# Four changes of order and three gate operations on GpSimd in an mLSTM and two-layer MoE kernel

## The chip, the cores and the metric

The kernel runs on one core of a Trainium2 chip. The metric is the device time of one execution, in microseconds. The engines are called PE (TensorE), DVE (VectorE), ACT (ScalarE), POOL (GpSimd) and SP (SyncE, here only a queue that issues DMAs).

## The reference

Three layers follow one another on 1536 tokens of width 320 (2 sequences of 768, 8 heads of 40).

```python
# 1. mLSTM: a recurrence over the 768 steps, for every sequence and head
m_new = np.maximum(f_gate[:, :, t] + m, i_gate[:, :, t])
f_stab = np.exp(f_gate[:, :, t] + m - m_new)
i_stab = np.exp(i_gate[:, :, t] - m_new)
C = f_stab * C + i_stab * outer(vt, kt);  n = f_stab * n + i_stab * kt
y[:, :, t] = sigmoid(o_gate) * (C @ qt) / np.maximum(np.abs(n @ qt), 1.0)
# 2. a dense layer with softplus, 320 -> 2048 -> 320
h = x @ w_in;  g = np.maximum(h, 0.0) + np.log1p(np.exp(-np.abs(h)));  x = g @ w_out
# 3. eight experts, one per token, 320 -> 1024 -> 320
e_idx = np.argmax(x @ w_gate, axis=1);  gate_w = softmax(x @ w_gate)[e_idx]
eom = sigmoid(x @ w_output_gate)
out[mask] = gate_w[mask] * eom[mask, e] * (np.maximum(x[mask] @ w1[e], 0.0) @ w2[e])
```

Matmul operands are split in a high and a low part, so most products are three passes over PE.

## The kernel before

The program is recorded by a planner (`Weaver`, L45). Every piece of work is a generator that names, before each group of instructions, the engine it wants (P, A, V, G or S for PE, ACT, DVE, POOL, SP; "AV" for either of two) or the events that it waits for. The planner keeps an estimated clock for each engine, takes the task that can start first (ties by `rank`), and so writes one fixed order of instructions per engine. A change of one engine letter, price or rank can therefore move instructions far away. On the chip each engine runs its own queue in that order and waits for semaphores.

The stages are:

- *Gates* (`gates`, L384). The recurrence of m is a scan along 768 steps on 80 partitions (16 heads, copied at three places). `gates(0, 0, 1)` does chunk 0 (128 steps) and `gates(1, 1, NCH)` chunks 1 to 5, 640 columns at once. With tiles fg, ig and mm it computes fg + mm(t-1) - mm(t), clips it, sums it per chunk into acum, splits acum of chunks 0 and 1 in bf16 parts (tile scratch), computes ig - mm, and transposes both on PE into gps, whose exponentials (gts) are the per-token weights.
- *Attention* (`chunk`, L518), per chunk c and sequence b. ap is the mask of decays, sp the scores, abc the decayed scores (a product on DVE), pv the values (v on POOL scales them), kv the update of the carried state cst, qc what the state gives. num and sm hold the quotient on DVE; POOL multiplies it with the sigmoid (y), PE transposes it (xp) and it becomes the high and low x of the dense layer.
- *Dense layer* (`up1`, `softplus`, `down1`). ph = x w_in per block of 256 tokens and strip of 128 hidden columns, three exponent/log steps on ACT (ab), g, gh and gl, then acc = g w_out. Strips are done in three legs (4, 4 and 8 of 16) so that PE has this work under attention. Weights come as 64-bit words and are put together on DVE (wta), then split (win, wou).
- *Routing* (`route`, L879, `take_row`, L850) of each 256-token block when its acc is complete: the row is added up, its columns 256 to 320 are copied behind it, PE transposes it (x2tp, x2T) and makes the logits (lg). Small DVE operations on tile rsm find the expert; a one-hot gives rank and totals on PE; newp, more_p, cum, room, base place every token in a slot of 128 rows. POOL scatters the rows to DRAM (`scatter`, an indirect DMA).
- *Between the layers*. `fence` (L1219) lets a POOL memset and a DVE copy on tile pad follow the scatters, before the low parts of w2 (w2s) may be written. `get_meta` (L1253) transposes the experts of the slots to one row (esp), casts it to integers (into pad), and PE loads them in registers. `load_rows` reads the slots back on SP's queue (yac, srow), followed by the last w2raw and the next weights.
- *Experts* (`slots`, `up2`, `post`, `down2`). 15 slots of 128 rows, four quarters of the hidden width: ph, hr (ReLU), tp (transposes), flat and hl (high and low part), yp, and the sum yac on DVE. In the last quarter each slot's yac is sent out by an indirect DMA on POOL (out_dram).

PSUM buffers come from rings: `bank` (4 buffers, 2 of them given to the ph ring at the end of attention), `bank_h`, `bank_y`. Nearly every instruction is recorded by one helper, so its line in the profile is L195; rows are told apart by tile names.

## Time and profile before

| what | value |
|---|---|
| median of 3 runs | 457.0 us (455.26 to 460.16) |
| the profiled execution, whole | 456.22 us |
| its span, first to last instruction | 454.5 us |
| PE, DVE, ACT, POOL busy | 94%, 73%, 68%, 29% of the span |
| granted TensorE clock, mean | 0.956 of full speed |
| DMA | 63.49 MB, mean 140 GB/s |

Times in the trace count from the first instruction. A row of a timeline gives start, duration, engine, operation, the tiles written and read, their shapes, and in brackets how long the engine was idle before it and whom it waited for. The profile's instruction spans overlap by some 0.07 us on DVE. A granted clock of 0.50 is 1.2 GHz, 1.00 is 2.4 GHz.

### The profile page before, as it was taken

The page shows a single profiled execution, that of the slowest core. Times are in us where ns is not written, and L with a number is a line of the kernel's source. Part 1 is how long each engine was busy: PE and PEld are TensorE (multiplying, and loading weights), DVE is VectorE, ACT ScalarE, POOL GpSimd, SP SyncE. Part 2 cuts the span into 40 slices and gives each one's busy share as a digit, 9 for nine tenths or more (in the row PEclk, how much of TensorE's full clock was granted, in tenths as well). Part 3 has the DMA queues.
Part 4 walks back from the last instruction along what each step waited for, and adds up shares of the span by engine and source line. Part 5 has one row for each costly group of instructions (what it writes and reads, how often), then busy time and mean ns, then how long its engine had stood idle before and what let it go on. Part 6 is the DMA issues. An engine that isn't in the chain of part 4 may idle for free.

```text
span 454.5 us, 10149 instructions
## 1 busy us (share of the span) xinstructions
PE 425.6 (94%) x3189; PEld 404.0 (89%) x3189; DVE 332.8 (73%) x866; ACT 307.8 (68%) x881; POOL 133.9 (29%) x220
## 2 busy tenths in 40 slices
PE   8669999999979999999999999859999999999994
PEld 7557989999969999999999999717899999999993
DVE  3897888788995999855756656575569659769742
ACT  2549688888857998876867867445673773774430
POOL 3255476466131330010201101114023033051273
PEclk9676999999997999999999999969999999999998
DMA  8859645799147421100100100019146817726021
GB/s 291 343 173 316 201 144 186 218 338 273 67 150 283 157 95 60 59 0 2 36 2 36 36 1 36 36 64 357 46 120 206 290 36 207 271 68 201 26 103 51
DMA packets 31205, 63.49 MB, mean 140 GB/s; under 512 B 3516, under 2 KB 16063, under 8 KB 31152
## 3 DMA queue, kind: packets, MB, share of 16 engines
q1 hardware_dynamic: 29664, 58.46, 39.4%
q0 software_dynamic: 1488, 4.35, 2.6%
q8 instruction: 30, 0.49, 0.4%
q14 instruction: 23, 0.19, 0.1%
HBM read 54.64 MB, written 8.65 MB: 139 GB/s over the span
## 4 chain that ended last, share of the span: by engine, by line
PE 79%; DVE 8%; ACT 7%; issue 3%; DMA 2%; POOL 1%; SPq 0%; POOLq 0%; DVEq 0%; ACTq 0%
PE ph L195 31%; PE acc L195 17%; PE yp L195 10%; PE pv L195 4%; PE sp L195 4%; PE tp L195 3%; DMA w2raw<-in_w_dram 2%; PE kv L195 2%; PE lg L195 2%; ACT ab L195 2%; PE qc L195 2%; PE heat L195 2%; DVE w2s L195 1%; DVE wta L195 1%; ACT w2s L195 1%
## 5 line engine op out<-in xcount | busy, mean ns | idle before, releaser
L195 ACT ACTIVATE ab<-ab 128x256 f32<-128x256 f32 x192 | 77.7, 419 | 2.3
L195 DVE SCALAR_TENSOR_TENSOR g<-ph,ab 128x256 f32<-128x256 f32 x96 | 39.9, 419 | 24.8 <-ACT ab L195 24.2
L195 PE MATMUL ph<-w1s,flat 128*128 x300 | 56.3, 304 | 1.0 <-DVE w1s L195 0.6
L195 PE MATMUL acc<-win,gh 128*128 128x320 f32 x240 | 56.5, 321 | 0.5 <-ACT gh L195 0.5
L195 POOL TENSOR_TENSOR w1s<-w1raw,w1s 64x256 fp32r<-64x256 f32 x32 | 29.2, 938 | 89.3 <-ACT w1s L195 89.3
L195 PE MATMUL yp<-w2s,flat 128*128 x240 | 53.8, 312 | 0.5 <-ACT flat L195 0.5
L195 DVE TENSOR_TENSOR gl<-g,gh 128x256 fp32r<-128x256 f32 x96 | 45.7, 484 | 9.6 <-ACT gh L195 8.5
L195 ACT ACTIVATE ab<-ph 128x256 f32<-128x256 f32 x96 | 36.4, 381 | 18.0 <-PE ph L195 17.7
L195 PEld LDWEIGHTS ph<-w1s,flat 128*128 128x128 f32 x300 | 43.3, 188 | 2.0 <-ACT flat L195 0.9
L195 ACT CAST gh<-g 128x256 fp32r<-128x256 f32 x96 | 38.2, 403 | 7.4 <-DVE g L195 6.7
L195 PE MATMUL ph<-win 128*128 128x256 f32 x250 | 41.8, 291 | 0.0
L195 ACT ACTIVATE hr<-ph 128x256 f32<-128x256 f32 x60 | 23.1, 386 | 27.3 <-PE ph L195 25.9
L195 PEld LDWEIGHTS yp<-w2s,flat 128*128 128x128 f32 x240 | 39.7, 188 | 0.7 <-ACT flat L195 0.7
L195 DVE TENSOR_TENSOR hl<-tp,flat 128x256 fp32r<-128x256 f32 x60 | 25.2, 421 | 20.7 <-ACT flat L195 20.5
L195 PEld LDWEIGHTS acc<-win,gh 128*128 128x128 f32 x240 | 39.1, 191 | 1.2 <-ACT gh L195 1.0
L195 POOL DMA_INDIRECT rows<-row,rsm x12 | 12.6, 1050 | 93.3 <-ACT ab L195 55.6
L195 PE MATMUL acc<-win,gl 128*128 128x320 f32 x120 | 37.6, 314 | 0.0
L195 ACT CAST w2s<-w2raw 128x640 fp32r<-128x640 f32 x32 | 22.4, 727 | 22.0 <-PE yp L195 21.2
L195 PE MATMUL yp<-w2s,hl 128*128 x120 | 37.2, 310 | 0.0
L195 PEld LDWEIGHTS ph<-win 128*128 128x128 f32 x250 | 35.1, 194 | 0.5 <-issue 0.2
L195 PE MATMUL ph<-w1s,x2l 128*128 x180 | 33.5, 294 | 0.0
L195 PE MATMUL acc<-wou,gh 128*128 128x320 f32 x144 | 32.8, 313 | 0.3 <-ACT gh L195 0.3
(190 smaller groups left out, 1087.8 us busy)
## 6 DMA issues: line engine op xcount, KB each, us to landing
w1raw<-in_w_dram SPq DMA_DIRECT2D x32, 384.0 KB, 4.5
wra<-in_w_in_dram SPq DMA_DIRECT2D x16, 704.0 KB, 4.3
w2raw<-in_w_dram SPq DMA_DIRECT2D x32, 320.0 KB, 3.3
abc<-abc_dram SPq DMA_DIRECT2D x4, 1024.0 KB, 8.2
rows<-pad SPq DMA_DIRECT2D x19, 194.0 KB, 6.0
kT<-in_k_t_dram SPq DMA_DIRECT2D x6, 512.0 KB, 5.2
qT<-in_q_t_dram SPq DMA_DIRECT2D x6, 512.0 KB, 6.1
kn<-in_k_dram SPq DMA_DIRECT2D x5, 416.0 KB, 7.3
```

Of the source, the lines that this page charges most:

```text
L195: return fn(*args, **kw)
```

## The change

Five edits:

1. In `gates`, for chunks 1 to 5 (n = 1), the add and the subtract on fg and the subtract on ig go from DVE to POOL. Chunk 0 stays on DVE.
2. In `take_row`, for the last block, the copy of columns 256 to 320 becomes an add of 64 columns on DVE ahead of the row add.
3. In `route`, the negated maximum and the exponentials on ACT (`weigh`) come ahead of the one-hot; rank and totals get a PSUM tile rk of their own, and the warm matmuls of the last block take a buffer of `bank_y`.
4. `fence` also waits for an event that `get_meta` signals when the cast into pad is recorded.
5. In `up2`, in the last quarter, the last three of the 15 slots have rank 7.0 instead of 9.0, so that they come ahead of `down2` (rank 8).

```diff
@@ gates
-        yield "V"
-        DVE.tensor_tensor(out=fg[:, p0:t1], in0=fg[:, p0:t1], in1=mm[:, p0 - 1:t1 - 1], op=ALU.add)
-        yield "V"
-        DVE.tensor_tensor(out=fg[:, p0:t1], in0=fg[:, p0:t1], in1=mm[:, p0:t1], op=ALU.subtract)
+        eng = (DVE, "V") if n == 0 else (POOL, "G")
+        yield eng[1]
+        eng[0].tensor_tensor(out=fg[:, p0:t1], in0=fg[:, p0:t1], in1=mm[:, p0 - 1:t1 - 1], op=ALU.add)
+        yield eng[1]
+        eng[0].tensor_tensor(out=fg[:, p0:t1], in0=fg[:, p0:t1], in1=mm[:, p0:t1], op=ALU.subtract)
...
-        yield "V"
-        DVE.tensor_tensor(out=ig[:, t0:t1], in0=ig[:, t0:t1], in1=mm[:, t0:t1], op=ALU.subtract)
+        yield eng[1]
+        eng[0].tensor_tensor(out=ig[:, t0:t1], in0=ig[:, t0:t1], in1=mm[:, t0:t1], op=ALU.subtract)
@@ take_row
+            if last:
+                DVE.tensor_tensor(out=row[:, t, DM:CCOL], in0=acc[:, 256:DM], in1=row[:, t, 256:DM], op=ALU.add)
             DVE.tensor_tensor(out=row[:, t, 0:DM], in0=acc, in1=row[:, t, 0:DM], op=ALU.add)
-            yield "AV"
-            copy(row[:, t, DM:CCOL], row[:, t, 256:DM])
+            if not last:
+                yield "AV"
+                copy(row[:, t, DM:CCOL], row[:, t, 256:DM])
@@ route
+    def weigh(le, ex, nmx, ssum, done):
+        yield "A"
+        for t in range(TPB):
+            ACT.activation(out=ex[:, t], in_=le[:, t], func=AF.Exp, bias=nmx[:, t:t + 1], accum_out=ssum[:, t:t + 1])
+        W.signal(done)
...
-        lg, ev = yield from bank.get([P, 64], F32, "lg")
+        lg, lg_ev = yield from bank.get([P, 32], F32, "lg")
...
+        rk, ev = yield from bank.get([P, 24], F32, "rk")
+        rank = rk[:, 0:T8].rearrange("p (t e) -> p t e", e=E)
+        tot = rk[:, T8:T8 + E]
...
         tt(lt, le, bc(mx, E), ALU.is_lt)
+        DVE.tensor_scalar(out=nmx, in0=mx, scalar1=-1.0, scalar2=None, op0=ALU.mult)
+        W.add(after(W.cur.out, weigh(le, ex, nmx, ssum, have_ssum)), 0.9)
...
-            warm, wev = yield from bank.get([P, 4, P], F32, "warm")
+            warm, wev = yield from bank_y.get([P, 4, P], F32, "warm")
...
-        DVE.tensor_scalar(out=nmx, in0=mx, scalar1=-1.0, scalar2=None, op0=ALU.mult)
         tt(sel, lo_, ohb, ALU.mult)
         yield "V"
         DVE.tensor_reduce(out=oge, in_=sel, axis=AX.X, op=ALU.add)
+        yield [have_ssum]
         yield "A"
-        for t in range(T2):
-            ACT.activation(out=ex[:, t], in_=le[:, t], func=AF.Exp, bias=nmx[:, t:t + 1], accum_out=ssum[:, t:t + 1])
         ACT.activation(out=ef, in_=oge, func=AF.Exp, scale=-1.0)
+        W.signal(lg_ev)
@@ fence, get_meta
-        yield [scattered]
+        yield [scattered, have_meta]
...
         DVE.tensor_copy(out=meta, in_=esp)
         W.signal(ev)
+        W.signal(have_meta)
@@ up2
                     yield [slot_ready[s]]
+                W.cur.rank = 7.0 if qn == NQ - 1 and s >= NS - 3 else 9.0
```

What the planner makes of it is shown at three places.

DVE, from the scan of chunks 1 to 5 on (mm is the scan's result, abc the decayed scores, sm and num the quotient of chunk 0, wta the weights put together). Before:

```order
L195 SCALAR_TENSOR_TENSOR mm<-fg,mm,ig 80x640
L195 SCALAR_TENSOR_TENSOR wta<-wra,wta 128x704
L195 TENSOR_TENSOR fg<-fg,mm 80x640
L195 SCALAR_TENSOR_TENSOR wta<-wra,wta 128x704
L195 TENSOR_TENSOR abc<-sp,abc 128x4x128 x2
L195 TENSOR_TENSOR fg<-fg,mm 80x640
L195 TENSOR_SCALAR fg<-fg 80x640
L195 TENSOR_TENSOR abc<-sp,abc 128x4x128
L195 SCALAR_TENSOR_TENSOR acum<-scratch,fg 80x128 x5
L195 TENSOR_SCALAR sm<-pv 128x8
L195 TENSOR_TENSOR abc<-sp,abc 128x4x128
```

The same place on DVE in the changed kernel:

```order
L195 SCALAR_TENSOR_TENSOR mm<-fg,mm,ig 80x640
L195 SCALAR_TENSOR_TENSOR wta<-wra,wta 128x704 x2
L195 TENSOR_TENSOR abc<-sp,abc 128x4x128 x3
L195 TENSOR_SCALAR sm<-pv 128x8
L195 TENSOR_SCALAR fg<-fg 80x640
L195 SCALAR_TENSOR_TENSOR sm<-pv,sm 128x8
L195 TENSOR_TENSOR abc<-sp,abc 128x4x128
L195 RECIPROCAL sm<-sm 128x8
L195 SCALAR_TENSOR_TENSOR acum<-scratch,fg 80x128 x5
L195 TENSOR_TENSOR num<-pv,sm 128x8x40
L195 TENSOR_SCALAR sm<-pv 128x8
L195 CAST scratch<-acum 80x128
```

The two fg operations are gone, three score products stand together, and the clip of fg (TENSOR_SCALAR) stands behind an operation on pv.

POOL at the same time (v_217 and v_219 are the values of the two sequences in chunk 0, v_282 or v_284 and v_318 the same with the decay to the chunk's end, which kv needs; y is the product with the sigmoid; win a low part of weights; v_422 and on belong to chunk 1). Before:

```order
L195 COPY v_219<-gts 128x8
L195 TENSOR_TENSOR v_282<-v_217,sm 128x328
L195 TENSOR_TENSOR v_318<-v_219,sm 128x328
L195 TENSOR_TENSOR win<-wta,win 64x128 x2
L195 TENSOR_TENSOR y<-num,y 128x320
L195 TENSOR_TENSOR v_422<-vn_87,gts 128x8x40
L195 COPY v_422<-gts 128x8
L195 TENSOR_TENSOR v_423<-vn_87,gts 128x8x40
L195 COPY v_423<-gts 128x8
L195 TENSOR_TENSOR y<-num,y 128x320
```

The same place on POOL in the changed kernel:

```order
L195 COPY v_219<-gts 128x8
L195 TENSOR_TENSOR fg<-fg,mm 80x640
L195 TENSOR_TENSOR v_284<-v_217,sm 128x328
L195 TENSOR_TENSOR fg<-fg,mm 80x640
L195 TENSOR_TENSOR v_318<-v_219,sm 128x328
L195 TENSOR_TENSOR win<-wta,win 64x128
L195 TENSOR_TENSOR ig<-ig,mm 80x640
L195 TENSOR_TENSOR win<-wta,win 64x128
L195 TENSOR_TENSOR y<-num,y 128x320 x2
L195 TENSOR_TENSOR v_436<-vn_87,gts 128x8x40
```

The fg operations stand ahead of the v products, ig between the weights, and the second y has moved ahead of chunk 1's values.

DVE behind the last routing (rem, esl are the routing's last results, esp the slots' experts, the 1x1 copy is the fence's). Before:

```order
L195 SCALAR_TENSOR_TENSOR esl<-rsm,esl 128x1
L195 TENSOR_TENSOR rem<-rem,cum 128x1
L195 COPY pad<-pad 1x1
L195 TENSOR_TENSOR w2s<-w2raw,w2s 128x2x320
L195 CAST pad<-esp 1x256
```

The same place on DVE in the changed kernel:

```order
L195 SCALAR_TENSOR_TENSOR esl<-rsm,esl 128x1
L195 TENSOR_TENSOR rem<-rem,cum 128x1
L195 CAST pad<-esp 1x256
L195 COPY pad<-pad 1x1
L195 TENSOR_TENSOR w2s<-w2raw,w2s 128x2x320 x7
```

The cast has moved ahead of the fence's copy and of the w2s subtractions.

In the last slots, PE's order before ends with ph (4 of 8 matmuls), yp, the other 4 ph, transposes, yp; in the changed kernel the last ph is complete ahead of the last four yp groups.

## Rows read from the trace of the kernel before

**Rows 1.** The page's busy times: us, share of the span, instructions.

```profile
PE 425.6 (94%) x3189; PEld 404.0 (89%) x3189; DVE 332.8 (73%) x866; ACT 307.8 (68%) x881; POOL 133.9 (29%) x220
```

**Rows 2.** Busy time by stage: us, engines (instructions), granted clock, DMA share, GB/s.

```profile
20.00:30.00 10.00, 8.54 (x68) 8.25 (x66) 9.54 (x25) 6.06 (x15) 2.47 (x2) 0.84 0.49 177
30.00:40.00 10.00, 7.06 (x33) 5.22 (x33) 9.00 (x17) 7.75 (x29) 5.79 (x8) 0.50 1.06 333
...
120.00:140.00 20.00, 16.95 (x121) 16.43 (x120) 18.15 (x38) 12.60 (x33) 3.95 (x4) 0.87 0.31 97
...
150.00:200.00 50.00, 49.88 (x381) 49.68 (x380) 46.01 (x95) 44.47 (x124) 8.92 (x12) 1.00 0.23 76
```

**Rows 3.** Timeline of DVE, 15 to 34 us.

```profile
15.67 1.35 DVE L195 TENSOR_TENSOR fg<-fg,mm 80x640 f32<-80x640 f32 x1
...
17.75 1.27 DVE L195 TENSOR_TENSOR abc<-sp,abc 128x512 f32<-128x512 f32 x2
...
27.99 0.81 DVE L195 TENSOR_TENSOR ig<-ig,mm 80x640 f32<-80x640 f32 x1
...
33.05 0.48 DVE L195 TENSOR_TENSOR num<-pv,sm 128x320 f32<-128x320 f32 x1
```

**Rows 4.** POOL: its timeline, 28 to 35 us, and two tiles (ns min/median/max).

```profile
28.12 2.07 POOL L195 TENSOR_TENSOR win<-wta,win 64x128 fp32r<-64x128 f32 x1 [5.72 <-ACT win L195]
30.27 0.81 POOL L195 TENSOR_TENSOR y<-num,y 128x320 f32<-128x320 f32 x1
...
33.62 1.38 POOL L195 TENSOR_TENSOR y<-num,y 128x320 f32<-128x320 f32 x1
...
L195 POOL TENSOR_TENSOR win<-wta,win x10: 451/799/2067, 21.8 to 189.0; 64x128 fp32r<-64x128 f32 x10
...
L195 POOL TENSOR_TENSOR w1s<-w1raw,w1s x32: 732/792/1256, 142.7 to 410.1; 64x256 fp32r<-64x256 f32 x32
```

**Rows 5.** Timeline of PE, the head and the end of attention.

```profile
18.52 1.65 PE L195 MATMUL kv<-v,kn 128*104 128x82 f32 x8 [4.37 <-issue]
19.97 2.95 PE L195 MATMUL pv<-v,abc 128*128 128x123 f32 x16
...
40.05 1.43 PE L195 MATMUL ph<-win 128*128 128x256 f32 x5
...
135.54 0.90 PE L195 MATMUL xp<-ident,y 128*128 128x128 f32 x3 [3.02 <-POOL y L195]
```

**Rows 6.** Timeline of DVE, the last block's placement.

```profile
297.82 0.17 DVE L195 TENSOR_TENSOR newp<-lg,room 128x8 f32<-128x8 f32 x1 [0.47 <-ACT rsm L195]
...
299.36 0.17 DVE L195 CAST rsm<-rsm 128x2 uint32<-128x2 f32 x1
```

**Rows 7.** Timelines of DVE, PE, SP and ACT, between routing and slots.

```profile
303.61 0.41 DVE L195 CAST pad<-esp 1x256 int32<-1x256 f32 x1
...
308.48 1.00 PE L195 MATMUL xslot<-ident,yac 128*128 128x128 f32 x6
...
309.12 0.40 SPq L195 DMA_DIRECT2D w2raw<-in_w_dram  x1
...
317.06 0.73 ACT L195 CAST w2s<-w2raw 128x640 fp32r<-128x640 f32 x1 [0.85 <-DMA w2raw<-in_w_dram]
```

**Rows 8.** Timelines of PE and POOL, the last slots.

```profile
441.35 0.99 POOL L195 DMA_INDIRECT out_dram<-yac,tki  x1 [0.30 <-issue]
442.35 0.47 PE L195 MATMUL yp<-w2s,flat 128*128 x2
444.28 0.98 POOL L195 DMA_INDIRECT out_dram<-yac,tki  x1 [1.94 <-DVE yac L195]
446.86 0.44 PE L195 MATMUL tp<-ident,hr 128*128 128x128 f32 x2 [0.53 <-ACT hr L195]
447.76 0.56 PE L195 MATMUL yp<-w2s,flat 128*128 x2 [0.46 <-ACT flat L195]
...
449.94 0.98 POOL L195 DMA_INDIRECT out_dram<-yac,tki  x1 [2.10 <-DVE yac L195]
```

More of the change, by code (lines that the diff above doesn't have):

```diff
@@ L897, in route @@
         T2, T8 = TPB, TPB * E
+        have_ssum = Event()
         small, small_ev = yield from sm_ring.get([P, 8 * T2 + 6 * T8 + 4 * E], F32, "rsm")
@@ L908, in route @@
         le, lo_ = lgv[:, :, 0:E], lgv[:, :, E:2 * E]
-        rank = lg[:, 2 * T8:3 * T8].rearrange("p (t e) -> p t e", e=E)
-        tot = lg[:, 3 * T8:3 * T8 + E]
+        rk, ev = yield from bank.get([P, 24], F32, "rk")
+        rank = rk[:, 0:T8].rearrange("p (t e) -> p t e", e=E)
+        tot = rk[:, T8:T8 + E]
         yield "V"
@@ L1216, in mlstm_moe_kernel @@
     flag = pad[0:1, 0:2]
-    clear, last_placed = Event(), Event()
+    clear, last_placed, have_meta = Event(), Event(), Event()
     def fence():
-        yield [scattered]
+        yield [scattered, have_meta]
         yield "G"
@@ L1249, in mlstm_moe_kernel @@
     meta = pad[0:1, 64:64 + 2 * P].bitcast(I32)
-    have_meta, turned_over = Event(), Event()
+    turned_over = Event()
     evals = {}
```

## The prediction

> **What bounds the kernel now.** I read the page's busy times first: PE works 425.6 of the 454.5 us span [rows 1], so all that any change of order can win lies in PE's 29 idle us and in the stretches where its clock is low. The table by stage says where those are [rows 2]. From 20 to 40 us PE is busy 8.54 and 7.06 of each 10 us, at a granted clock of 0.84 and 0.50 of full speed, while DVE is busy 9.54 and 9.00: the head (gates, first chunks) is DVE's. From 120 to 140 us, where attention ends, PE lacks 3.05 us. From 150 to 200 it is busy 49.88 of 50: there a change of order is worth nothing, but what was won earlier is carried through. Two short serial places follow: the routing of the last block with the start of the expert slots (292 to 310 us), and the last slots.
>
> The change is weighed at those four places. The planner writes one order for the whole program, so the gates on another engine reshuffle everything up to the end of attention; behind the last routing the rows on PE differ only among the first slots and the last three.
>
> **Head: the three gate operations.** DVE loses one add of 1.35 us and two 80x640 operations of 0.81 us [rows 3], 2.97 us in all. POOL has no 640-element row. Its smallest times for 128 and 256 elements are 0.451 and 0.732 [rows 4], 2.2 ns an element, so 0.73 + 384 x 0.0022 = 1.58 us each, an estimate; the nearest stretched row is 2.07 us for 128 elements, 4.6 times the smallest, so 7.3 us is the other end. What is behind them? On POOL the first batch's v product now stands between the add and the subtract, the second's behind it; on DVE the max over fg waits for POOL's subtract, and behind it stand the fourth score product, the scans and all of chunk 1's gates. In the old order the add started at 15.67; from there POOL takes 1.58 + 0.8 (a v product, taken as the undisturbed 128x320 row of 0.81) + 1.58, to 19.6.
>
> In DVE's new rows three score products stand where the add stood, so they start 1.28 earlier than 17.75 (the add without its overlap), at 16.5, and the second ends at 17.7. PE's new rows begin with pv instead of the kv that idled 4.37 us until 18.52 [rows 5]. PE therefore starts 0.8 earlier, and this pv (2.95 us in the old trace) ends near 20.6. The max stands behind an operation on that pv, so POOL's 19.6 is hidden, with 1.0 us to spare. But DVE, done with its products at about 18.3, now idles 2.3 us for pv: of its 2.97 us only 0.7 is left. That is the low end of the gain, if the head stays DVE's.
>
> The high end comes from the second batch's y product on POOL. It ran from 33.62 to 35.00, because the division that feeds it came at 33.05 on DVE, behind the acum casts, weight conversion and the ig subtraction. In the new rows that division stands before the casts, and POOL runs both y products back to back: the first ended at 31.08, the second can end at 31.9, or 32.5 if it is stretched to 1.38 again. That is 3.1 or 2.5 us earlier, and PE's first ph (40.05) needs it. With PE's 0.8 on top the high end is 3.9. I take 2.5, the stretched y row, since DVE's conversions fill that stretch in both orders. Between 45 us and the end of attention PE has so little idle time that I let it carry.
>
> At the end of attention [rows 5] PE idles 3.02 us for the last y. The new rows put about as much work before the last transpose xp, but less between the last pv and it, and between that pv's sum and its division DVE has six operations fewer. I cost this at zero, with 3 us either way as bounds: the gap gone, or doubled.
>
> **Routing of the last block.** In the old order the first operation of the placement (newp) idled 0.47 us on the ACT exponentials and started at 297.82 [rows 6]. In the new one ACT starts them after the negated maximum, while DVE still makes the one-hot, and rank and totals have a PSUM bank of their own. The placement can start once the rank matmuls are done and the output gate is reduced, 0.75 us earlier. Against it stands the 64-column add in front of the row add; the small DVE rows here last 0.17 and cost about 0.1 in a stream, and the ACT copies that it replaces were beside PE's transposes. Net 0.65 to 0.75 us; I take 0.7. The same edits in blocks 0 to 4 lie under PE's 49.88 of 50, and the further PSUM bank is taken when the block's transposes have left theirs, so I count nothing there. Scatter, the read-back of the rows and everything that SP issues behind them move by the same 0.7.
>
> **Fence.** In the old order DVE's cast of the slot experts (pad<-esp) ran at 303.61 [rows 7], behind the fence's copy, which waits for the scatter issue, and behind one w2s subtraction. PE then loads the numbers, runs six warm matmuls and only then transposes slot 0 at 308.48. In the new rows the cast stands directly behind the routing, and could run near 301. The seven w2s subtractions still queue behind the fence's copy on DVE and move 0.7 with the scatter. PE would then be free before the rows land, and slot 0 would start about 2.0 earlier (0.7 from the scatter, 1.3 from the cast). What is late next: w2raw for expert 7, issued by SP behind all row loads at 309.12. ACT's cast of it waited 0.85 us and began at 317.06; it stands at the same place in ACT's queue, after slot 4's ReLU, with the next slots behind it. That landing moves only 0.7. I therefore count 0.7 for routing and fence together, and 2.0 as the other end, if PE finds enough work behind the block.
>
> **Last three slots.** The new rows take all ph products ahead of the last four yp groups. That removes PE's two waits of 0.53 and 0.46 us [rows 8]. But POOL issues each output with 0.99 busy and 0.30 between, 1.29 us apart, and it idled in the old order at 444.28. Now four outputs come together, and the first of them stands on DVE behind both hl subtractions. PE: 442.35 (the old yp's place) plus eight ph (1.0), transpose, half a yp, transpose, half a yp ends near 444.7; ACT and DVE then finish the second hl near 445.2, the output's sum at 445.7, POOL 445.98. The fourth issue is at 445.98 + 3 x 1.29 = 449.85, against 449.94. So POOL takes the place of PE: I count zero, with 1.0 less and 0.3 more as bounds.
>
> **Sum.** The profiled execution took 456.22 us, 1.7 outside its span; it lies 0.8 under the median of 457.0 and inside the runs. 456.2 - 2.5 - 0.7 - 0 = 453.0.
>
> **Rivals.** *The head is given back.* PE reaches 45 us early, but the end of attention comes when DVE and ACT are done, and the gap of 3.02 grows by what was won. For it: PE has less work left behind the last pv. Against it: from 45 to 120 us PE was the busy engine. Only routing stays: 456.2 - 0.7 = 455.5.
>
> *More than forecast.* The head wins the high end, 3.9, since PE is busy earlier where its clock stood at 0.50, and the expert slots win 2.0 because the late w2raw blocks ACT while PE has slots in hand. For it: PE lost only some tenths at that block before. Against it: ACT's queue is in order. 456.2 - 3.9 - 2.0 = 450.3.
>
> *Slower: POOL's add is stretched.* The add now lies beside two weight operations of DVE, each with two SBUF inputs. The trace has such a case: the 128-element POOL subtraction at 28.12 took 2.07 us instead of 0.45 beside DVE's two-input operations [rows 4]. At that ratio the add takes 7.3 us and the subtract ends near 25.3, 4.7 after the pv for which DVE waits anyway; DVE's max, the fourth score product, and with it the second pv, the scans and chunk 1 are that much later. The head loses 4.7 - 2.5 = 2.2: 456.2 + 2.2 - 0.7 = 457.7. It decides for slower from a subtract that ends later than 23.8 (20.6 + 2.5 + 0.7). Against it: 640 elements last longer than the DVE work beside them, and the score products read PSUM. The Trainium skill speaks for it: GPSIMD Engine Reference, Key points, says that GpSimd shares its SBUF interfaces with VectorE and contends with instructions of two SBUF inputs. The 2.07 us row agrees; how far 640 elements are stretched no run here shows.
>
> *It does not do what it says:* the new order of the middle loses as much as the head wins, 456.2. I put it with the second case of no gain above.
>
> **Chances.** Forecast 0.50; head given back 0.22; more 0.16; stretched add 0.12. A measurement of this kernel tells about 1% from no change, 4.6 us of the median 457.0. Under 452.4 lie the case of more and, with one time in four, the forecast (its own range 451.3 to 455): 0.16 + 0.5 x 0.25 = 0.29 for faster. Over 461.6 lies only the far end of the stretched add with a gap that doubles, 0.05. Within 1%: 0.66. The range takes in the case of more nearly whole and the stretched add: 450.0 to 458.0.
>
> **What would show it.** Right: the first ph before 37.5 instead of 40.05 (score matmuls now stand behind it), and equal work done 2.5 earlier at 45 us; POOL's 80x640 rows of 1.6 to 2.5 us; newp without a wait for ACT and 0.75 closer to the row add; the pad cast near 301, slot 0 at 306.5 less the head's gain, ACT's wait for w2raw grown from 0.85 to about 2; the last four outputs 1.29 apart. Wrong: POOL rows of 80x640 above 4 us with DVE idle at the fg max, or an xp wait at the end of attention of 5 us or more.

## The result and the profile of the changed kernel

The changed kernel took 460.7 us (median of 19 runs, 457.71 to 465.01), the kernel before 456.27 (19 runs, 455.26 to 460.23). The ratio is 1.0091, 95% interval 1.0072 to 1.0111: 0.9% slower, where 0.7% faster was predicted (453.0 against 456.2), and outside the range of 450 to 458.

The two profiled executions have spans of 459.3 and 454.5 us. Where the 4.8 us arise, by the distance between marks that both traces have (starts, in us):

| stretch | before | changed | difference |
|---|---|---|---|
| start to the last block's row add | 291.69 | 295.12 | +3.43 |
| row add to newp (routing) | 6.13 | 5.64 | -0.49 |
| newp to slot 0's transposes (xslot) | 10.66 | 9.09 | -1.57 |
| xslot to the first yp | 27.39 | 29.87 | +2.48 |
| first yp to the last output's issue | 114.07 | 114.00 | -0.07 |
| last output's issue to the end | 4.56 | 5.58 | +1.02 |

The loss lies first of all ahead of the routing, in the stretch for which a gain of 2.5 was forecast. The page's busy times hardly moved against [rows 1]: the same work, done later.

```profile
PE 425.4 (93%) x3189; PEld 403.7 (88%) x3189; DVE 331.4 (72%) x865; ACT 308.0 (67%) x879; POOL 131.6 (29%) x223
```

The table by stage of the changed kernel, columns as in [rows 2]:

```profile
20.00:30.00 10.00, 7.82 (x63) 7.40 (x62) 8.09 (x25) 4.04 (x11) 1.99 (x2) 0.84 0.26 101
30.00:40.00 10.00, 7.17 (x35) 6.22 (x36) 8.26 (x15) 6.19 (x21) 7.47 (x23) 0.53 0.98 312
60.00:80.00 20.00, 18.44 (x154) 17.54 (x153) 18.87 (x40) 17.62 (x58) 9.51 (x17) 1.00 0.83 255
80.00:120.00 40.00, 40.00 (x331) 38.29 (x330) 28.76 (x68) 33.37 (x107) 20.41 (x34) 1.00 0.63 200
120.00:140.00 20.00, 16.21 (x121) 14.71 (x119) 19.05 (x41) 13.82 (x36) 3.69 (x5) 0.96 0.35 121
140.00:150.00 10.00, 10.00 (x63) 10.00 (x64) 8.80 (x15) 8.00 (x21) 3.26 (x3) 0.73 0.79 275
150.00:200.00 50.00, 49.92 (x380) 49.43 (x379) 45.74 (x94) 45.43 (x124) 10.53 (x13) 1.00 0.31 108
```

The same view of the kernel before, for the stretch that [rows 2] leave out:

```profile
80.00:120.00 40.00, 39.92 (x330) 38.41 (x331) 33.74 (x75) 34.97 (x110) 21.87 (x32) 1.00 0.81 250
```

From 80 to 120 us DVE is busy 28.76 us instead of 33.74. From 120 to 150 it has 27.85 instead of 24.71, and at the end of attention it is nearly full. PE lost 1.3 us more between 60 and 80 and 0.7 more between 120 and 140. From 140 to 150 its clock was 0.73 instead of 0.92, but over the whole of 120 to 150 it is 0.89 in both kernels.

How much of PE's work is done shows where the loss grows. The kernel before has started 240 of its 3189 matmuls by 45 us; the changed kernel starts its 240th 1.6 us earlier. At the count of 60 us it is level (0.1 earlier), at that of 80 us 0.8 later, of 120 us 1.6 later and of 150 us 2.8 later (small and large matmuls count alike here).

**Head.** The timelines of POOL, DVE, PE and ACT in the changed kernel:

```profile
14.36 2.09 POOL L195 TENSOR_TENSOR fg<-fg,mm 80x640 f32<-80x640 f32 x1 [3.02 <-ACT sm L195]
16.41 1.38 POOL L195 TENSOR_TENSOR v<-v,sm 128x328 f32<-128x328 f32 x1
17.76 1.53 POOL L195 TENSOR_TENSOR fg<-fg,mm 80x640 f32<-80x640 f32 x1
...
20.59 1.53 POOL L195 TENSOR_TENSOR ig<-ig,mm 80x640 f32<-80x640 f32 x1
```

```profile
14.20 3.00 DVE L195 SCALAR_TENSOR_TENSOR wta<-wra,wta 128x704 uint32<-128x704 uint32 x2
17.12 1.87 DVE L195 TENSOR_TENSOR abc<-sp,abc 128x512 f32<-128x512 f32 x3
21.70 0.17 DVE L195 TENSOR_SCALAR sm<-pv 128x8 f32<-128x8 f32 x1 [2.71 <-PE pv L195]
...
33.13 0.24 DVE L195 TENSOR_SCALAR gts<-gps 128x80 f32<-128x80 f32 x1 [1.36 <-ACT gts L195]
```

```profile
17.95 3.71 PE L195 MATMUL pv<-v,abc 128*128 128x123 f32 x16 [3.65 <-DVE abc L195]
...
36.14 1.44 PE L195 MATMUL ph<-win 128*128 128x256 f32 x5 [0.34 <-ACT win L195]
...
46.59 1.98 PE L195 MATMUL pv<-v,abc 128*128 128x123 f32 x16
...
66.84 0.93 PE L195 MATMUL kv<-v,kn 128*104 128x82 f32 x8 [1.56 <-POOL cst L195]
```

```profile
32.47 0.24 ACT L195 COPY y<-y 128x64 f32<-128x64 f32 x1 [1.55 <-POOL y L195]
32.73 0.36 ACT L195 ACTIVATE gts<-gps 128x80 f32<-128x80 f32 x2
```

DVE and PE in the kernel before:

```profile
30.39 0.24 DVE L195 TENSOR_SCALAR gts<-gps 128x80 f32<-128x80 f32 x1 [0.44 <-ACT gts L195]
```

```profile
46.59 1.88 PE L195 MATMUL pv<-v,abc 128*128 128x123 f32 x16
```

POOL's subtract ends at 19.29, and DVE waits for pv until 21.70, so the subtract is hidden. The add is not quite: the second of DVE's two wta operations beside it lasts 2.11 us (the median of the 32 is 0.88), the score products stand behind it, and PE's pv waits for the first of them. pv therefore ends near 21.7, where 20.6 was forecast. The first ph starts 3.9 us earlier than in [rows 5]. But DVE's use of chunk 1's gates (gts) now starts at 33.13, where it stood at 30.39 before, because its exponentials stand on ACT behind a copy of y that waits for POOL's y. Chunk 1's first pv starts at 46.59 in both kernels. So the dense layer is ahead and attention isn't; at 66.84 PE waits 1.56 us for the carried state that POOL scales (cst), where the kernel before idles 0.28 us in all from 60 to 80.

**End of attention**, on PE:

```profile
130.99 1.87 PE L195 MATMUL pv<-v,abc 128*128 128x123 f32 x16
...
138.52 0.90 PE L195 MATMUL xp<-ident,y 128*128 128x128 f32 x3 [2.75 <-POOL y L195]
139.99 1.43 PE L195 MATMUL ph<-xh,win 128*128 128x256 f32 x5 [0.57 <-ACT xh L195]
```

and before:

```profile
124.09 3.21 PE L195 MATMUL pv<-v,abc 128*128 128x123 f32 x28
```

The idle time is about that in [rows 5], but all of it stands 3.0 us later. The last pv row of the kernel before holds 28 matmuls, most of both sequences, so the two rows are compared by their ends: 132.86 instead of 127.30, 5.6 us later.

**Routing, fence, first slots**: DVE, PE, SP and ACT.

```profile
300.76 0.16 DVE L195 TENSOR_TENSOR newp<-rk,room 128x8 f32<-128x8 f32 x1
...
304.53 0.41 DVE L195 CAST pad<-esp 1x256 int32<-1x256 f32 x1 [0.89 <-PE esp L195]
```

```profile
309.85 1.14 PE L195 MATMUL xslot<-ident,yac 128*128 128x128 f32 x6 [1.23 <-DMA yac<-rows]
...
322.43 0.41 PE L195 MATMUL tp<-ident,hr 128*128 128x128 f32 x2 [1.74 <-DVE x2l L195]
```

```profile
312.45 0.48 SPq L195 DMA_DIRECT2D w2raw<-in_w_dram  x1
```

```profile
320.24 0.72 ACT L195 CAST w2s<-w2raw 128x640 fp32r<-128x640 f32 x1 [0.95 <-DMA w2raw<-in_w_dram]
```

Against [rows 6] newp has no wait for ACT. Against [rows 7] the cast into pad is 0.92 later in a kernel that is by then 2.83 later (the scatter at 303.22 instead of 300.39), and PE now waits for the rows themselves. The last w2raw is issued 3.3 us later than before, while slot 0 is only 1.4 later: what slot 0 won, the stretch up to the first yp gives back, and more (1.57 against 2.48).

**Last outputs**, on POOL, answering to [rows 8]:

```profile
449.85 0.99 POOL L195 DMA_INDIRECT out_dram<-yac,tki  x1 [3.80 <-DVE yac L195]
451.14 0.98 POOL L195 DMA_INDIRECT out_dram<-yac,tki  x1 [0.30 <-DVE yac L195]
452.43 0.98 POOL L195 DMA_INDIRECT out_dram<-yac,tki  x1 [0.30 <-issue]
453.72 0.98 POOL L195 DMA_INDIRECT out_dram<-yac,tki  x1 [0.30 <-DMA out_dram<-yac,tki]
```

PE's two waits are gone and its last matmul starts 1.6 us sooner after the first yp (111.31 instead of 112.90), but four outputs 1.29 apart end where the last one ended before.

### The profile page after: what moved, and what is told of

It is laid out like the page before. It is cut to its first block, busy times and chain, and to the rows that moved or that the text cites. A ratio compares the mean times of both kernels' runs of the same rounds, so it can differ in the third digit from the quotient of the medians.

```text
span 459.3 us, 10160 instructions
## 1 busy us (share of the span) xinstructions
PE 425.4 (93%) x3189; PEld 403.7 (88%) x3189; DVE 331.4 (72%) x865; ACT 308.0 (67%) x879; POOL 131.6 (29%) x223
## 4 chain that ended last, share of the span: by engine, by line
PE 70%; DVE 8%; DMA 8%; issue 6%; ACT 4%; POOL 2%; SPq 1%; POOLq 0%; DVEq 0%; ACTq 0%
PE ph L195 30%; PE acc L195 17%; PE yp L195 7%; PE pv L195 4%; PE sp L195 4%; DMA out_dram<-yac,tki 3%; PE tp L195 3%; DVE wta L195 2%; DMA wra<-in_w_in_dram 2%; DMA w2raw<-in_w_dram 2%; PE qc L195 2%; ACT ab L195 1%; PE kv L195 1%; PE lg L195 1%; DMA og<-in_o_gate_dram 1%
## 5 line engine op out<-in xcount | busy, mean ns | idle before, releaser
L195 DVE TENSOR_TENSOR gl<-g,gh 128x256 fp32r<-128x256 f32 x96 | 44.0, 467 | 13.1 <-ACT gh L195 12.6
L195 PE MATMUL ph<-win 128*128 128x256 f32 x250 | 42.8, 293 | 0.3 <-ACT win L195 0.3
L195 DVE TENSOR_TENSOR hl<-tp,flat 128x256 fp32r<-128x256 f32 x60 | 25.2, 421 | 20.7 <-ACT flat L195 20.6
L195 PE MATMUL acc<-win,gl 128*128 128x320 f32 x120 | 37.5, 313 | 1.1 <-DVE gl L195 1.1
```

Source lines behind the costliest of these rows:

```text
L195: return fn(*args, **kw)
```

## The experiments

The record gives a chip number with each experiment. On chips 1 (g1 to g4) and 15 (p_0023, b_0096), marked a, the kernel before took 456.1 to 456.4 us; on chips 2 (r5_lastchunk and the runs named e_), 6 (l_after, l_best, r235, p_0021) and 5 (after_again, r5_low, b_0100, best2), marked b, it took 462.7 to 463.7. The first result has no chip number and is marked a by its time. Every ratio is to the kernel before on the same chip. Ratios from different chips can be compared only roughly: the changed kernel itself has 1.0091 in one place and 1.0144 in another. Two columns are from the traces: the busy time of PE and of DVE from 40 to 120 us, of 80.

| run | | ratio | 95% interval | PE | DVE |
|---|---|---|---|---|---|
| the kernel before | | 1 | | 79.64 | 66.07 |
| the changed kernel | a | 1.0091 | 1.0072 to 1.0111 | 78.09 | 62.97 |
| after_again | b | 1.0144 | 1.0098 to 1.0190 | 78.45 | 62.79 |
| g1_gates | a | 1.0143 | 1.0094 to 1.0192 | 78.45 | 62.53 |
| g2_rest | a | 1.0037 | 1.0014 to 1.0059 | 79.71 | 66.74 |
| g3_order | a | 1.0125 | 1.0104 to 1.0147 | 78.46 | 63.44 |
| g4_engine | a | 1.0016 | 0.9991 to 1.0041 | 79.64 | 65.50 |
| e_routefence | b | 0.9982 | 0.9958 to 1.0006 | 79.64 | 66.05 |
| e_rank | b | 0.9990 | 0.9965 to 1.0014 | 79.56 | 66.33 |
| r5_lastchunk | b | 1.0107 | 1.0046 to 1.0168 | 78.45 | 60.63 |
| l_after | b | 1.0174 | 1.0127 to 1.0220 | 79.03 | 62.39 |
| r5_low | b | 1.0119 | 1.0080 to 1.0158 | 78.45 | 60.87 |
| r235 | b | 1.0229 | 1.0199 to 1.0258 | 77.39 | 68.68 |
| p_0021 | b | 1.0037 | 1.0017 to 1.0057 | 79.43 | 65.29 |
| p_0023 | a | 1.0090 | 1.0055 to 1.0126 | 77.35 | 63.39 |
| b_0100 | b | 1.0066 | 1.0033 to 1.0100 | 80.00 | 62.66 |
| b_0096 | a | 1.0109 | 1.0070 to 1.0149 | 80.00 | 62.28 |
| e_w2 | b | 0.9966 | 0.9947 to 0.9984 | 79.66 | 65.42 |
| l_best | b | 1.0040 | 1.0014 to 1.0065 | 79.52 | 64.22 |
| best2 | b | 0.9927 | 0.9890 to 0.9964 | 79.62 | 65.37 |

Some runs also show how far a single trace can be trusted. Six kernels (the one before, g2_rest, e_routefence, e_rank, e_w2, best2) have one order on PE up to the first block's logits; the changed kernel, after_again and g1_gates have the other. The first ph comes at 38.8 to 40.7 us in the six and at 36.1 to 37.6 in the three, the last xp of attention at 134.3 to 136.1 and 138.5 to 140.2, the last block's row add at 290.6 to 292.5 and 295.1 to 297.3. These ranges do not overlap, so the loss ahead of the routing goes with the order; its size is known to some 2 us.

**Which edit costs the time?** g1_gates is the kernel before with edit 1 alone, g2_rest the changed kernel without it, e_routefence edits 2 to 4 alone, e_rank edit 5 alone.

```diff
@@ g2_rest, against the changed kernel
-        eng = (DVE, "V") if n == 0 else (POOL, "G")
+        eng = (DVE, "V")
@@ e_routefence, further
-                W.cur.rank = 7.0 if qn == NQ - 1 and s >= NS - 3 else 9.0
+                W.cur.rank = 9.0
```

> The kernel before with only the three gate operations priced and issued on GpSimd (edit 1); routing, fence and last slots as before. Its PE order is that of the changed kernel up to the second routing. Theory A (the whole loss is made in attention by edit 1): the last y transpose comes near 138.5 us instead of 135.5, and the run is 3 to 4.5 us slower than before, so 459.5 to 461. Rival B (the loss is made behind attention, by routing, fence or the last slots): within 1 us of before, 455.5 to 457.5.

> The changed kernel with the three gate operations back on VectorE: edits 2 to 5 alone. Theory A: the last y transpose is back at 135.5 us; the routing wins 0.5 us (newp without a wait for ACT, against the 64-column add), the start of the slots gives it back at the late w2raw, and the end of the run may lose 1 us to outputs that land together: 455.5 to 457.5. Rival B: these edits carry the loss, 459 to 461. Step of the prediction: 0.7 faster than before, 455.6.

> Routing and fence edits alone (2 to 4): gates on VectorE and last slots as before. Step of the prediction: 0.7 us faster than before, 455.7. Rival from the trace of the changed kernel (the gain of 1.5 us at slot 0 is lost again at the last w2raw, whose issue comes with the scatter): the same as before, 456 to 457, with slot 0 about 1 to 1.5 us earlier against the scatter, and the first yp no earlier than before.

> The kernel before with edit 5 alone: the last three slots at rank 7.0 in the last quarter. Step of the prediction: PE ends about 1 us earlier, but four outputs then come together on GpSimd at 1.29 us each, so the last output is issued at the same time within 0.3 us and the run is the same as before, 456 to 457. Rival: the burst of outputs also lands later (the changed kernel's profile shows 5.6 us from the last issue to the end instead of 4.6): 457 to 458.

Edit 1 alone costs 1.4%: the whole loss and more. Edits 2 to 4 alone and edit 5 alone lie within 0.2% of the kernel before, and 1 lies inside both intervals. The parts do not add up: g2_rest is 0.4% slower, although its halves are not, and beside edit 1 the same four edits leave a smaller ratio than edit 1 alone (1.0091 against 1.0143, though the intervals overlap a little). The excess of g2_rest is not explained, and its profiled execution (456.39 us) does not have it: there block 0's first logits start at 210.37 instead of 209.76, where the order of PE has not changed yet, and the end comes at the same time. Part of the excess of edit 1 alone is seen in the routing. From the row add to newp its trace takes 7.23 us (g3_order below 7.55), at a granted clock of 0.50 (1.2 of 2.4 GHz) from some 2 us behind the row add; in both traces PE had stood idle for 2.26 us, waiting for ACT's gh, until 0.9 us before the row add. The changed kernel, in which no wait of PE there is above 0.6, takes 5.64, with the clock at 0.95 from 2 to 4 us behind the row add.

**The engine, or the order that the planner writes for it?** The two are separated by telling the planner one engine and using the other. In g3_order the planner books the three operations on POOL, in its rows of order and at its price, and DVE executes them. In g4_engine it books them on DVE, and POOL executes them.

```diff
@@ g3_order
+        eng = (DVE, "V") if n == 0 else (Priced(W, nc.vector, "G"), "G")
@@ g4_engine
+        eng = (DVE, "V") if n == 0 else (Priced(W, nc.gpsimd, "V"), "V")
```

> The planner is told that the three operations are on GpSimd, so that PE and ACT keep exactly the order of the run with edit 1 alone, but they are issued on VectorE, where they stand at the places that this plan gives them. Theory A1 (it is the order of the later chunks, with the second batch's scores late, that costs): the last y transpose stays near 138.5 and the time stays 3 to 4.5 us over before. Rival A2 (GpSimd's own durations, 2.1 and 1.5 us, and what waits for them cost the time): with the operations back on VectorE at 0.8 to 1.35 us the loss goes, within 1 us of before.

> The other half: the three operations are issued on GpSimd, but the planner prices them as VectorE operations, so that PE and ACT keep exactly the order of the kernel before up to the end. Theory A1: the engine alone costs little; VectorE is freed of 3 us in the head, and the run is between 2.5 us faster (the head's gain is carried) and the same as before. Rival A2: GpSimd's durations make the head late, and the run is 2 to 4 us slower than before.

g3_order has PE's and ACT's order of g1_gates and loses 1.25% with nothing executed on POOL. g4_engine has PE's and ACT's order of the kernel before and POOL's work, and its time doesn't differ. So it is the order, not the engine. And g4_engine shows something more: three operations taken off the busiest engine of the head won nothing. Its first ph starts at 41.32, against 40.05. DVE in its head:

```profile
14.64 3.00 DVE L195 SCALAR_TENSOR_TENSOR wta<-wra,wta 128x704 uint32<-128x704 uint32 x2
...
19.77 1.01 DVE L195 TENSOR_SCALAR fg<-fg 80x640 f32<-80x640 f32 x1 [0.93 <-POOL fg L195]
...
21.30 3.18 DVE L195 TENSOR_TENSOR_SCAN acum<-scratch,fg 80x128 f32<-80x128 f32 x5
```

In the kernel before the same rows took 1.73 (0.86 and 0.88), 0.49 and 1.89 us. Beside POOL's operations they are 3.1 us longer in all, and DVE waits 0.93 for POOL's subtract: what was taken off DVE, 2.97 us, comes back as longer rows and a wait. The last xp stands at 137.50, 2.0 later than before, yet the row add is only 0.9 later and the run no slower: the last xp alone does not tell the loss.

**Which place in the order?** Four repairs of the changed kernel at the end of attention: the last chunk's tasks ahead of the dense layer (r5_lastchunk); the low parts of weight strips 6 to 11 subtracted on POOL in the old place of the order, since DVE is full there (l_after); both (r5_low); strips 4 to 7 ahead of chunk 4's tasks (r235). after_again is the changed kernel itself on chip b.

```diff
@@ r5_lastchunk, r5_low
-        rank = 0 if c == 0 else 2 + 0.1 * c
+        rank = 0 if c == 0 else 2 + 0.1 * c if c < NCH - 1 else 1.9
@@ l_after, r5_low
-        vsub(place(n)[:, HIGH:WIDE], t[:, P:HIGH], place(n)[:, P:HIGH].bitcast(F32))
+        (Priced(W, nc.gpsimd, "V") if 6 <= n < 12 else DVE).tensor_tensor(
+            out=place(n)[:, HIGH:WIDE], in0=t[:, P:HIGH], in1=place(n)[:, P:HIGH].bitcast(F32), op=ALU.subtract)
@@ r235
-RANKS = [1] * 4 + [2.45] * 4 + [2.75] * 8
+RANKS = [1] * 4 + [2.35] * 4 + [2.75] * 8
```

> The changed kernel with one number more: the tasks of the last chunk (masks, scores, carried state, values) get rank 1.9 instead of 2.5, so that ties with the dense layer's strips (rank 2) go to them. On PE the second sequence's last scores, carried-state product and values then stand ahead of strips and accumulations that stood in front of them. Theory A (the loss is made by that place in the order: the second sequence's last pv began at 130.99 in the changed kernel, 124.09 before): the last y transpose comes at 135.5 or earlier, and the run is 2 to 4 us faster than the changed kernel, 456.5 to 458.5. Rival (the loss is made earlier, in the head or in the middle chunks, and the end only shows it): still 460 to 461.

> The changed kernel with its order untouched on PE and ACT; only the 128x576 low-part subtractions of weight strips 6 to 11 (0.75 us each on VectorE, four of them between 118 and 143 us) are issued on GpSimd at the same place in the program. Theory C (VectorE enters the end of attention with a backlog of weight strips, 3 us less done by 120 us than before, and is busy 19.05 of 20 us there): the last y transpose comes 1.5 to 3 us earlier than 138.5 and the run is 1 to 2.5 us faster than the changed kernel, 458 to 459.5 where before is 456.4. Rival D (the end is set by PE's own order of matmuls): the last y transpose and the time stay within 0.7 us.

> The changed kernel with the rank of weight strips 4 to 7 at 2.35 instead of 2.45, so that ties with the tasks of chunk 4 (2.4) go to the strips: they are converted earlier, about 10 to 20 us before the end of attention. Theory C (VectorE's backlog of strips): VectorE has done about 3 us more by 120 us, the end of attention is 2 to 3 us earlier and the run is 1.5 to 3 us faster than the changed kernel. Rival D: the work moved forward delays the chunks of attention instead, and the time stays within 1 us or rises.

> The changed kernel as it is, to have its ratio on the same chip as the kernels beside it. If chips do not matter: 1.007 to 1.012 of the kernel before. If the ratio of the changed kernel is another here, the ratios of r5_lastchunk, l_after, p_0021 and r235 must be read against that, not against 1.0091.

> The changed kernel with the last chunk's tasks at rank 1.9 and the low-part subtractions of weight strips 6 to 11 on GpSimd, the order kept. If the loss at the end of attention needs both repairs (TensorE's order there, and a full VectorE): 1.5 to 3 us faster than the changed kernel, a ratio of 1.003 to 1.006, and the first logits of the last block by 296. If it is the plan as a whole and neither repair binds: as r5_lastchunk, 1.0107, or slower, as l_after was.

None recovers the loss. after_again came out above the 1.007 to 1.012 that was expected of it. Against its 1.0144, r5_low, on the same chip, and r5_lastchunk may have won some tenths of a per cent; their intervals overlap its interval, and r5_low is no better than r5_lastchunk. In r5_lastchunk the last xp comes at 137.09, where 135.5 or earlier was expected. l_after, with PE's and ACT's order of the changed kernel, has it at 138.91 and is no faster (1.0174). r235 does what it should on DVE and is the slowest of all:

```profile
80.00:120.00 40.00, 38.35 (x298) 36.11 (x297) 33.84 (x70) 32.48 (x104) 23.96 (x35) 0.96 0.80 256
```

DVE has its 33.8 us back, PE has lost 1.65, and the last xp of attention comes at 143.12. A single place that would have to be mended was not found.

**A property of the move, or of the plan that comes out?** If the loss belonged to the three operations, it should not depend on small changes of a price. p_0021 and p_0023 are the changed kernel with the planner's price of the three operations 5% lower and higher. b_0100 and b_0096 are the kernel *before* with the price of VectorE operations of 640 elements 4% and 8% lower. No operation changes its engine in any of them.

```diff
@@ p_0021 (p_0023: 0.0023)
-                                0.00175 if n in (320, 328, 164) else 0.0022)
+                                0.00175 if n in (320, 328, 164) else 0.0021 if n == 640 else 0.0022)
@@ b_0100 (b_0096: 0.00096)
-                                    else 0.00104)
+                                    else 0.00100 if n == 640 else 0.00104)
```

> The changed kernel, with the planner's price for the three GpSimd operations 5% lower (0.0021 instead of 0.0022 us an element; nothing else differs, and the same instructions are issued on the same engines). The planner writes another order from the head on. Theory E (the loss belongs to the one order that this price gave, not to the operations on GpSimd): the time moves by more than 1.5 us to either side of the changed kernel. Rival F (any plan with these operations on GpSimd loses about the same): within 1 us of the changed kernel.

> The changed kernel with the planner's price of the three 640-element operations on GpSimd 5% higher (0.0023 us an element in place of 0.0022); no instruction changes its engine. If the loss is the particular plan: another time than the changed kernel's 1.0144 on this chip, by more than 0.3% to either side, as p_0021 was with 1.0037. If p_0021 was faster because a lower price is the truer one: 1.0144 or more here. The three operations' own time as the cause would leave it at 1.0144.

> The kernel before with one number of the planner changed: the price of a VectorE operation of 640 elements 0.00100 us an element in place of 0.00104; no instruction changes its engine, only the order. If the size of the loss is a matter of which plan the planner happens to write: the time moves by more than 0.3% to either side, and the time of the last xp of attention moves with it. If the plan is robust against its prices and the loss came from the three moved operations as such: within 0.2%.

> The kernel before with the planner's price of a VectorE operation of 640 elements at 0.00096 us an element in place of 0.00104 (913 lines of TensorE's order differ). If the plan of the kernel before is a good one among many: slower by 0.3 to 1.5%, as b_0100 was by 0.66%. If b_0100 was one bad plan and most are alike: within 0.3%.

5% on one price takes back more than half of the loss (p_0021 has 1.0037, the changed kernel 1.0091 or 1.0144; its interval lies below both). 5% to the other side (p_0023, 1.0090) is another time than 1.0144, as the plan theory expected, but none other than 1.0091; it decides nothing between the two. Nor is the lower price the truer one: at 0.0022 the planner books 0.12 + 640 x 0.0022 = 1.53 us, which is what the two undisturbed rows took. The two plans of the kernel before say most: without any operation moved they are 0.7% and 1.1% slower. Its own plan is better than these two neighbours, and an edit that makes the planner write another one can lose by that alone what edit 1 lost. The place differs: the last xp was expected to move with the time, but in b_0100 it stands at 135.65, as before, and the row add 3.1 later.

What do the slow plans have in common? In the table above every run with PE at 79.4 us or more and DVE at 64.2 or more has a ratio of at most 1.004, and each of the others 1.0066 or more. Both limits were chosen afterwards, with the ratios in view. The traces of b_0096 and p_0021 from 80 to 120 us show the two sides:

```profile
80.00:120.00 40.00, 40.00 (x328) 37.94 (x327) 27.38 (x66) 32.51 (x105) 20.54 (x33) 1.00 0.69 215
```

```profile
80.00:120.00 40.00, 40.00 (x332) 38.20 (x331) 34.70 (x75) 34.99 (x111) 22.76 (x34) 1.00 0.84 265
```

In b_0096, as in the changed kernel, DVE stands idle in the middle of attention and is full at its end. In the changed kernel one such delay can be read directly. The words of the first strip that goes to wou are put together on DVE (wta) and cast on ACT; before, DVE then ACT:

```profile
70.56 0.89 DVE L195 SCALAR_TENSOR_TENSOR wta<-wra,wta 128x704 uint32<-128x704 uint32 x1
...
88.37 0.51 DVE L195 TENSOR_SCALAR wta<-wra 128x704 uint32<-128x704 uint32 x1
```

```profile
84.54 0.77 ACT L195 CAST wou<-wta 128x704 fp32r<-128x704 f32 x1
```

and in the changed kernel:

```profile
76.75 0.84 DVE L195 SCALAR_TENSOR_TENSOR wta<-wra,wta 128x704 uint32<-128x704 uint32 x1
...
113.86 0.51 DVE L195 TENSOR_SCALAR wta<-wra 128x704 uint32<-128x704 uint32 x1
```

```profile
108.12 0.76 ACT L195 CAST wou<-wta 128x704 fp32r<-128x704 f32 x1
```

The cast stands 13.1 us behind the finished words in the one order and 30.5 in the other, and the next strip begins only behind it, at 113.86 instead of 88.37. Its conversion then falls into the stretch in which DVE finishes attention. That this delay is the cause was not shown: p_0021 has its first wou cast at 107.17 as well, and r235, which has it at 87.59, lost elsewhere.

**The late w2raw and the last outputs.** e_w2 is e_routefence with the last w2raw issued on SP right behind the first five row loads. l_best adds l_after's edit to it. best2 adds to e_w2 a part of edit 5: only the second half of the last slot's ph comes ahead of the yp groups.

```diff
@@ e_w2, load_rows
             else:
+                if not w2_sent:
+                    w2_sent.append(1)
+                    yield from load_w2(0, E - 1)
                 row, ev = yield from right["raw"].get([P, 1, ROW], F32, "srow", users=2)
...
-        yield from load_w2(0, E - 1)
@@ best2, up2
+                    if n == 4 and qn == NQ - 1 and s == NS - 1:
+                        W.cur.rank = 7.0
```

> Routing and fence edits alone (2 to 4; gates on VectorE, last slots as before), and SP issues the last w2raw behind the first five row loads instead of behind all eight. Theory (the last w2raw is what is late next): ACT's wait for it and PE's wait for the slot behind it are gone, the gain of 1.5 us between scatter and slot 0 is carried, 1 to 2.5 us faster than the run without that move and 1 to 2 us faster than before, 454.5 to 455.5. Rival (PE has other work there, or the rows for the last slots come late instead): no difference to the run without it.

> Routing and fence edits with the last w2raw issued behind the first five row loads (gates on VectorE, last slots as before), and the low-part subtractions of strips 6 to 11 on GpSimd in an unchanged order. Theory C: the 3.0 us of PE before the last y transpose are also VectorE's queue, so 1 to 2 us more than the 1.5 us that the earlier w2raw won: 453 to 454.5 where before is 456.4. Rival D: as without the subtractions, 454.5 to 455.5.

> e_w2 (edits 2 to 4 with the last slot's raw second weights issued behind the first five row loads) and, of edit 5, the second half of the last slot's hidden products at rank 7.0. If edit 5's gain on TensorE's end carries to the output here: 0.5 us faster than e_w2, a ratio of about 0.9955, with TensorE's two waits of about half a microsecond near the end gone. If the last outputs queue on GpSimd as in the changed kernel: as e_w2, 0.9966.

In e_w2 the load is issued at 305.82, 2.7 us ahead of e_routefence's 308.55, and ACT no longer waits for it:

```profile
315.24 0.72 ACT L195 CAST w2s<-w2raw 128x640 fp32r<-128x640 f32 x1
```

From xslot to the first yp it takes 28.18 us, e_routefence 29.14, the changed kernel 29.87. The interval of its ratio, 0.9947 to 0.9984, lies below 1, but overlaps that of e_routefence (0.9982): the 1 us is seen in the traces, and not shown in the time. l_best is slower: in the new rows POOL's subtractions of wou stand before attention's last y, and PE's wait there grows to 4.11 us. best2 is the fastest kernel of this study, 0.7% below the kernel before (its interval and e_w2's overlap a little). It differs from e_w2 only in PE's last 18 matmuls, and of PE's two waits there one (0.53) is gone and the other (0.46) stays. Its last output doesn't queue on POOL but waits for the sum on DVE:

```profile
456.12 0.98 POOL L195 DMA_INDIRECT out_dram<-yac,tki  x1 [1.27 <-DVE yac L195]
```

It is issued 2.26 us behind the output before it, in e_w2 3.08. That is about 0.8 us; the difference of the two ratios is 1.8 us of 456, on two chips, and the rest of it is not shown to be the edit's.

## Why the prediction was wrong

- *Head, -2.5.* Mechanism as told in the main, and POOL's rows too: the estimate of 1.58 us met 1.53 where undisturbed and 2.09 for the add. DVE's idle time was forecast at 2.3 and came to 2.71. The first ph at 36.14 met "before 37.5", but the term was over-sized: equal work was done 1.6 earlier at 45 us, not 2.5, since part of those 3.9 us is ph moved ahead of the score matmuls. What failed is the step "between 45 us and the end of attention PE has so little idle time that I let it carry". PE being busy there says that the order fits its work, and this order was rewritten. In the new rows PE idles 1.9 us from 40 to 120 instead of 0.4, DVE does 3.1 us less, and the gain of 1.6 us at 45 us is a loss of 1.6 at 120 and of 2.8 at 150. g3_order shows that the order alone does it (1.0125 with nothing on POOL), g4_engine that the engine alone does not (1.0016); which place in the order costs most stays open.
- *End of attention, 0 within 3 either way.* The price was looked for in PE's wait for the last y, which hardly changed (2.75 against 3.02). Neither of the two signs of being wrong came, a wait of 5 us there or POOL rows above 4. The loss came in front of it: the last pv ends 5.6 us later. Both terms together were forecast at -2.5 and are +3.4 at the row add. The rival "the head is given back" had the direction, but with a bound of 0 at that place; "it does not do what it says" put the loss of the middle at what the head wins. No case held a middle that loses some 6 us, because the new order of some 80 us of attention was weighed at its two ends alone.
- *Stretched add.* The add was stretched by 1.37, not by 4.6: 0.56 us on POOL. No rival counted what it does to DVE, whose second wta operation lasted 2.11 us instead of 0.88 and held up the score products. That did not decide the run: g4_engine has it and is no slower, g3_order lacks it and loses. The Trainium skill (GPSIMD Engine Reference, Key points) has GpSimd contend with VectorE instructions of two SBUF inputs. The trace agrees, since the add ran beside DVE's wta operations, which read wra and wta, and both sides grew.
- *Routing, -0.7.* Right in its form; -0.49 measured. Newp lost its wait and came 0.74 us closer to the logits, and the 64-column add cost 0.25 in front. Where the clock stayed at 1.00 up to the logits the stretch took 5.53 to 5.54 us with these edits and 6.01 to 6.02 without; where it fell to 0.50 before that, 6.06 to 6.16 with them (g2_rest, e_routefence, best2), so the clock there is worth as much as the edits.
- *Fence, 0 more, 2.0 as the other end.* Right in its mechanism, not in its size: slot 0 came 1.57 earlier against newp, and the late w2raw and PE's wait behind it took back more (2.48), so that the two stretches together cost 0.9 where 0 was forecast. ACT's wait for w2raw, forecast at about 2, is 0.95 here and 2.11 in e_routefence. By the traces of e_w2 and e_routefence the load's place is about 1 us of the stretch to the first yp.
- *Last slots, 0.* Right, and for the reason given: POOL's outputs, 1.29 apart, took PE's place. The 1.02 us behind the last issue were not foreseen and are not explained: of the ten traces with edit 5 six have 5.6 to 6.2 us there and four (g2_rest, r5_low, l_after, r235) 4.4.

## What to carry to other kernels

Where a planner writes the order, an edit's own price and the price of the new order are two things: run the edit once in the old order and once as the order alone (as g4_engine and g3_order do), and change a price by some per cent, to see how far the time moves with no operation moved. Here that was 0.7 and 1.1%, as much as was forecast for all five edits together (0.7%) or more. An operation that goes to another engine can lengthen the rows that stay behind: compare the durations of the neighbours too, not only of the row that moved. A wait that is removed is worth only what the next instruction in the same in-order queue allows: move the load that is late next together with it, and look at the output queue before PE is made to end earlier.

## What the hardware showed

The twelve traces marked b have a stop some 20 us ahead of the end that the traces marked a do not show. In best2, on PE, ACT and DVE:

```profile
438.55 0.69 PE L195 MATMUL tp<-ident,hr 128*128 128x128 f32 x2 [5.85 <-ACT hr L195]
```

```profile
438.11 0.66 ACT L195 ACTIVATE hr<-ph 128x256 f32<-128x256 f32 x2 [13.45 <-remote]
```

```profile
435.22 0.55 DVE L195 SCALAR_TENSOR_TENSOR yac<-yp,cc,yac 128x320 f32<-128x320 f32 x1 [3.76 <-remote]
```

The ReLU on ACT stood although PE's ph had ended near 432.7, and the profile names no releaser in the kernel; in the kernel before on chip a the longest wait of ACT in that stretch is 7.19 us, for PE's ph. What stops the engines is open. From the first yp to the last output the b traces take 120.5 to 122.1 us and the a traces 113.6 to 114.1, so the 6 to 8 us by which the b runs are longer lie in that stretch. Also unexpected was how little POOL suffers beside DVE on long rows, 2.09 against 1.53 us for 640 elements, where 128 elements took 2.07 instead of 0.45 in [rows 4], and how much DVE does: 2.11 against 0.88 us for wta beside POOL's add, and in g4_engine 1.68 against 0.39 for one 128-element scan beside POOL's ig subtract. In both cases the DVE row lasts about as long as what was left of POOL's row plus its own time, 1.35 + 0.88 and 1.40 + 0.39, an estimate from the rows' starts and ends.
